# Turning the gate-scaled combine weights by block transposes on VectorE and DMAs

## The chip, the cores and the metric

One core of a Trainium2 chip. The time is device microseconds of one execution, taken as the median of several. The engines are named as the profile names them: PE (TensorE, matmuls), PEld (its weight loads, which run beside the matmuls), DVE (VectorE), ACT (ScalarE), POOL (GpSimd) and SP (SyncE), on whose queue nearly all DMAs are issued.

## What is computed

Three layers, one behind the other: attention with a compressive memory, a soft mixture of experts (32 slots), and a second mixture in which each of 8 experts sees all 2304 tokens, weighted by a balanced gate. The part that matters here, cut from the reference:

```python
# first mixture: combine weights c of 32 slots for each token
x = c @ slot_out                       # 2304 x 512
# second mixture
P = exp(x @ w_gate - max)              # 2304 x 8
for _ in range(8):                     # rows and columns balanced
    P /= P.sum(1); P /= P.sum(0); P *= N / E
for e in range(8):
    out += P[:, e:e+1] * (relu(x @ w1[e]) @ w2[e])
```

## The kernel before

The program runs in stages: attention with the first half of the first mixture (to about 260 us), the slots' experts (to about 320 us), and the second mixture, which takes the rest. Only this last stage is touched.

**What it multiplies.** Since x = c @ slot_out, x @ w1[e] is c @ (slot_out @ w1[e]), a product over 32 slots. prepare_a (L1037) makes slot_out @ w1[e] on TensorE, 32 matmuls per expert. split_a parts it into a rounded high part and the rest, and move_a (L1072) copies these with 16 DMAs of SP's queue into the four bands of 32 partitions of a4s[e]: high, low, high, low. Across it stands c4T (L793), 128 partitions by 2304 tokens: the combine weights c, turned, in the bands high, high, low, low. One matmul over 128 partitions so sums all four partial products.

**The gate.** P is never negative, so P * relu(c @ A) is relu((P c) @ A): the gate is applied by scaling c for each expert. For expert e, scale_c(e, u0, u1) (L1264) multiplies Cw (c with tokens on partitions: tile, slot) by column e of Pr on DVE into cP (L1267), rounds it on ACT to chi (L1272), copies chi twice into c4 (L1276) and writes the remainder cP - chi twice on DVE (L1277). turn_c (L1279) transposes each 128 x 128 tile of c4 on TensorE into a bank of PSUM (L1282), and store_c (L1286) copies the bank on ACT into c4T (L1287). One such step covers four tiles of 128 tokens (two units); the fifth of an expert covers two.

**Units and steps.** A unit is one expert e and 256 tokens u (9 units per expert, 72 in all; g = 9e + u). layer1(g) (L1091) makes the hidden values of a unit with 8 matmuls into the two banks l0 and l1. The second layer of a unit is done with seven products p1 to p7 on quarters of the matrices (the scheme of Strassen and Winograd) in the order p5, p1, p7, p6, p2, p3, p4; each product (L1392) is 12 matmuls at L1402 to L1404, three for each of four strips, high times high, high times low, low times high. hidden(g, k) (L1140) makes the operands: DVE the sums f (L1120) and the low parts a11l, a12l, a22l (L1133), ACT the rounded high parts (L1126), POOL the low parts s1l to s4l (L1137). collect (L1407) adds products from PSUM to accA, accB and accD on DVE (L1418). The products go to banks y0 to y4 in this order, all of one pool with three buffers, so a unit's y0 takes the bank that the unit before used for y2. p7 and p3 share y2, which accB collects. The first five units (RAW) do plain products instead.

**The order** is written out by hand (from L1476 on) for PE, DVE, ACT and POOL: unit by unit, seven steps k each; in a step come product(g, k), at k = 1 also layer1(g + 1), the collecting of the product of the step before, hidden(g + 1, k) for k > 1, and last the functions put `beside` step s = 7g + k (`at(u, k, f, ...)`). SP issues its DMAs in order as their waits allow. With v = 9(e - 1), the first unit of the expert before e, these stand beside the units: load_w1(e) at v, move_a(e) at v + 1, sums and splits of w2 (w_sum, w_hi, w_lo, mostly on POOL) from v + 2 to v + 9, and the steps of c in units v + 6 to v + 10 (L1342), with scale_c at k = 1, turn_c at k = 2, store_c at k = 3. layer1 of the expert's first unit, v + 9, is issued at k = 1 of unit v + 8.

sel (L1014) is a constant selection matrix that only expert 0 uses, in spread_a (L1061).

Of the kernel before, what the change touches and what calls it, by code (L numbers as in the profile page):

```python
# [8 lines left out]
F32 = mybir.dt.float32  # L9
BF16 = mybir.dt.bfloat16  # L10
F32R = mybir.dt.float32r
AF = mybir.ActivationFunctionType
ALU = mybir.AluOpType
# [8 lines left out]
def infini_attention_soft_moe_sinkhorn_moe(  # L22
# [15 lines left out]
    nc = tc.nc  # L38
    B, H, D, S = q.shape
    N, DM = out.shape  # L40
    E = moe2_w1.shape[0]
    FF = moe2_w1.shape[1] * moe2_w1.shape[4]
    NS = moe_phi.shape[2]
    SPE = NS // E
    P = 128
# [3 lines left out]
    KD = DM // P  # L49
# [4 lines left out]
    NTT = N // P  # L54
# [25 lines left out]
    ones = cst.tile([P, P], F32, name="ones")  # L80
# [31 lines left out]
    with ExitStack() as actx:  # L112
        def pool(nm, bufs=1):
# [13 lines left out]
            out=maskw[:, 3 * P :], in_=maskw[:, 3 * P :], compare_op=ALU.is_ge,  # L127
# [6 lines left out]
        for j in range(2):  # L134
            sl = maskt[64 * j : 64 * j + 64]
            nc.gpsimd.affine_select(
                out=sl, in_=sl, compare_op=ALU.is_ge,
# [6 lines left out]
        for i in range(QTB):  # L144
            pr = []
            for nm, w in (("qz", 3 * TAIL), ("qx", 2 * TAIL)):
                t = e2.tile([P, w], F32R, name=f"{nm}{i}")
# [5 lines left out]
        for i in range(2):  # L153
            t = ep[i].tile([P, 2, S], F32R, name=f"klz{i}")
# [77 lines left out]
        for c0, c1 in ((0, 2 * P), (2 * P, S)):  # L232
# [14 lines left out]
            out=gB[:, 1, :], in0=gB[:, 0, :], scalar1=-1.0, scalar2=1.0,  # L247
# [437 lines left out]
        def at(p, n, f, *args):  # L685

            fill.setdefault(3 * NT * p + n, []).append((f, args))
# [84 lines left out]
    with bctx:  # L772
# [20 lines left out]
        c4T = cst.tile([P, 2 * (OB[4] + TAIL)], F32R, tag="pB", name="c4T")  # L793
# [89 lines left out]
        with tc.manual_schedule(engines={mybir.EngineType.PE}):  # L883
            c4 = combine(0)
            first(0)
            for bb in range(1, B):
# [3 lines left out]
                c4 = combine(bb)  # L890
# [18 lines left out]
    mB = ctx.enter_context(tc.tile_pool(name="mB", bufs=1, reuse_waits="tile"))  # L909
# [5 lines left out]
    mD = ctx.enter_context(tc.tile_pool(name="mD", bufs=1, reuse_waits="tile"))  # L915
# [6 lines left out]
    NU = N // UT  # L922
# [80 lines left out]
    def w_lo(e, nm, i, g):  # L1003
# [7 lines left out]
    mD.tile([P, 16], F32, name="gap")  # L1011
    a4s = {0: mD.tile([P, FF], F32R, tag="a4", name="a4", bufs=2)}
    Cw = mD.tile([P, NTT, NS], F32, name="Cw")
    sel = mD.tile([P, 4, 160], F32R, name="sel")  # L1014
    nc.vector.tensor_scalar(
        out=sel.rearrange("p j c -> p (j c)"), in0=ones[:, 0:1].to_broadcast([P, 640]),
        scalar1=0.0, scalar2=None, op0=ALU.mult,
    )

# [8 lines left out]
    a2s, G = {}, {}  # L1028
# [142 lines left out]
    Pr = mB.tile([P, NTT, E], F32, name="Pr")  # L1171
# [2 lines left out]
    m1 = mS.tile([P, 1], F32, name="m1")  # L1174
    m2 = mS.tile([1, 1], F32, name="m2")

    def gate_slots():
        soB = G["soB"] = mB.tile([P, KD, 4, NS], F32, tag="c4", name="soB")
        nc.scalar.activation(out=soB, in_=soR.to_broadcast([P, KD, 4, NS]), func=AF.Copy)

    def gate_weights():
# [80 lines left out]
    cs_ = {}  # L1262

    def scale_c(e, u0, u1):  # L1264
        T0, n = 2 * u0, 2 * (u1 - u0)
        cP = mB.tile([P, 4, NS], F32, tag="cP", name="cP")[:, 0:n]
        nc.vector.tensor_tensor(  # L1267
            out=cP, in0=Cw[:, T0 : T0 + n], in1=Pr[:, T0 : T0 + n, e : e + 1].to_broadcast([P, n, NS]),
            op=ALU.mult,
        )  # L1270
        chi = mB.tile([P, 4, NS], F32R, tag="chi", name="chi")[:, 0:n]
        nc.scalar.activation(out=chi, in_=cP, func=AF.Copy)  # L1272
        c4 = cs_[e, u0] = mB.tile([P, 4, 4, NS], F32, tag="c4", name="c4")
        hb = chi.bitcast(F32).rearrange("p t (o s) -> p t o s", o=1).to_broadcast([P, n, 2, NS])
        cb = cP.rearrange("p t (o s) -> p t o s", o=1).to_broadcast([P, n, 2, NS])
        nc.scalar.activation(out=c4[:, 0:n, 0:2, :], in_=hb, func=AF.Copy)  # L1276
        nc.vector.tensor_tensor(out=c4[:, 0:n, 2:4, :], in0=cb, in1=hb, op=ALU.subtract)  # L1277
# [8 lines left out]
    def store_c(e, u0, u1):  # L1286
        nc.scalar.activation(  # L1287
            out=c4T[:, UT * u0 : UT * u1], in_=G["pc"][:, 0 : UT * (u1 - u0)], func=AF.Copy
        )


    side = {}

    def beside(s, f, *args):
        side.setdefault(s, []).append((f, args))
# [22 lines left out]
    def at(u, k, f, *args):  # L1318
        beside(7 * u + k, f, *args)

    def c_steps(v, e, u0, u1):
        at(v, 1, scale_c, e, u0, u1)
        at(v, 2, turn_c, e, u0, u1)
        at(v, 3, store_c, e, u0, u1)

    for k, u0, u1 in ((-1, 5, 7), (2, 7, 9)):
        for n, f in enumerate((scale_c, turn_c, store_c)):
            at(RAW - 1, k + n, f, 0, u0, u1)
    s = 1
# [9 lines left out]
        at(RAW - 1, 5 + i, w_lo, 0, "T3", i, "P")  # L1339
    for e in range(1, E):  # L1340
        v = NU * (e - 1)
        for i in range(5):  # L1342
            c_steps(v + 6 + i, e, 2 * i, min(2 * i + 2, NU))
        at(v, 0, load_w1, e, e % 2)
        at(v + 3 * (e == 1), 4, load_raw, e)

        at(v + 1, 3 + 2 * (e == 1), prepare_a, e)
        at(v + 1, 4 + (e == 1), split_a, e)
        at(v + 1, 5 + (e == 1), move_a, e)
        for i in range(2):  # L1350
            for n, nm in enumerate(("T1", "T2", "T4")):

                s = 29 + 4 * (3 * i + n) if e == 1 else 7 * (v + 2 + 3 * i + n) + 1
                beside(s, w_sum, e, nm, i, "P")
                beside(s + 2 - (e == 1), w_hi, e, nm, i)
                beside(s + 3 - (e == 1), w_lo, e, nm, i, "P")
            at(v + 6 + i, 2, w_sum, e, "T3", i, "P")
        for nm, k in (("B11", 2), ("T3", 4), ("B21", 6), ("B22", 8)):
            for i in range(2):
                at(v + 8, k + i, w_hi, e, nm, i)  # L1360
                at(v + 8, k + i + (nm[0] == "B" and nm[1] == "2"), w_lo, e, nm, i, "D" if nm == "B22" and i else "P")
# [114 lines left out]
    with tc.manual_schedule(engines={E_.PE, E_.DVE, E_.Activation, E_.Pool}):  # L1476
# [4 lines left out]
        gate_ident()  # L1481
        fill_sel()
        gate_slots()
        prepare_a(0)
        split_a(0)
# [18 lines left out]
        for g in range(len(units)):  # L1504
            nxt = g + 1 < len(units)
            for k in range(7):
                s = 7 * g + k
# [95 lines left out]
```

## Time and profile before

| | us |
|---|---|
| three runs | 1125.75, 1132.69, 1137.99 |
| median | 1132.69 |
| span of the profiled execution | 1137.8 |
| PE busy in it | 1089.2 |
| DVE busy | 858.2 |
| POOL busy | 663.0 |
| ACT busy | 643.7 |

The span runs from the first to the last instruction of the profiled execution. Its own time isn't given beside it; the span lies 0.2 us under the longest of the three runs. Matmuls are pipelined: the profile's duration of one runs from its start to a modelled end and overlaps the next, so what a matmul costs is read from the distance of starts.

### The profile page before, as it was taken

The page shows a single profiled execution, that of the slowest core. Times are in us where ns is not written, and L with a number is a line of the kernel's source. Part 1 is how long each engine was busy: PE and PEld are TensorE (multiplying, and loading weights), DVE is VectorE, ACT ScalarE, POOL GpSimd, SP SyncE. Part 2 cuts the span into 40 slices and gives each one's busy share as a digit, 9 for nine tenths or more (in the row PEclk, how much of TensorE's full clock was granted, in tenths as well). Part 3 has the DMA queues.
Part 4 walks back from the last instruction along what each step waited for, and adds up shares of the span by engine and source line. Part 5 has one row for each costly group of instructions (what it writes and reads, how often), then busy time and mean ns, then how long its engine had stood idle before and what let it go on. Part 6 is the DMA issues. An engine that isn't in the chain of part 4 may idle for free.

```text
span 1137.8 us, 24481 instructions
## 1 busy us (share of the span) xinstructions
PE 1089.2 (96%) x9229; PEld 991.8 (87%) x9229; DVE 858.2 (75%) x1881; ACT 643.7 (57%) x1392; POOL 663.0 (58%) x605
## 2 busy tenths in 40 slices
PE   6979999987999999999999999999999999999998
PEld 4757777774367799999999999999999999999998
DVE  7868898885157467778778877877887787788776
ACT  6868878861153557546555644655564465546442
POOL 4423333300064388587777857776785777678665
PEclk9989999997999999999999999999999999999999
DMA  6567687437932004001300400130040022000111
GB/s 154 162 175 232 198 233 225 116 106 282 419 121 93 1 2 149 20 1 67 95 9 1 149 20 1 56 103 11 1 149 20 1 70 90 10 2 6 52 57 56
DMA packets 42644, 105.70 MB, mean 93 GB/s; under 512 B 8224, under 2 KB 18592, under 8 KB 38432
## 3 DMA queue, kind: packets, MB, share of 16 engines
q1 hardware_dynamic: 42096, 104.07, 28.8%
q8 instruction: 73, 1.20, 0.4%
q14 instruction: 43, 0.35, 0.1%
q10 hardware_dynamic: 432, 0.09, 0.0%
HBM read 95.74 MB, written 4.72 MB: 88 GB/s over the span
## 4 chain that ended last, share of the span: by engine, by line
PE 77%; DVE 7%; DMA 5%; ACT 4%; issue 3%; POOL 2%; SPq 0%; DVEq 0%; ACTq 0%; POOLq 0%
PE y L1402 18%; PE y L1403 18%; PE y L1404 18%; PE l L1096 5%; PE po L447 4%; PE y L1369 2%; PE pt L410 2%; DMA wm<-in_moe_w_dram 2%; PE pa L1043 1%; DMA kd<-in_k_dram 1%; ACT sm L371 1%; DMA w<-in_moe_w_dram 1%; PE pc L1282 1%; DVE sm L367 1%; DMA qp<-in_q_dram 1%
## 5 line engine op out<-in xcount | busy, mean ns | idle before, releaser
L1120 DVE SCALAR_TENSOR_TENSOR f<-l,f 128x512 f32<-128x512 f32 x268 | 184.0, 687 | 61.1 <-ACT a11h L1126 53.1
L1137 POOL TENSOR_TENSOR s1l<-f,s1h 128x512 fp32r<-128x512 f32 x67 | 90.2, 1347 | 157.0 <-ACT s1h L1126 157.0
L1418 DVE TENSOR_TENSOR accA<-accA,y 128x512 f32<-128x512 f32 x125 | 85.4, 683 | 44.3 <-PE y L1404 43.9
L1126 ACT ACTIVATE a12h<-l 128x512 fp32r<-128x512 f32 x72 | 43.2, 600 | 99.2 <-PE y L1404 90.0
L1137 POOL TENSOR_TENSOR s4l<-f,s4h 128x512 fp32r<-128x512 f32 x67 | 87.4, 1305 | 15.8 <-PE y L1403 10.4
L1418 DVE TENSOR_TENSOR accB<-accB,y 128x512 f32<-128x512 f32 x125 | 85.5, 684 | 6.7 <-PE y L1404 0.2
L1137 POOL TENSOR_TENSOR s3l<-f,s3h 128x512 fp32r<-128x512 f32 x67 | 87.1, 1301 | 0.0
L1137 POOL TENSOR_TENSOR s2l<-f,s2h 128x512 fp32r<-128x512 f32 x67 | 86.9, 1297 | 0.0
L1116 ACT ACTIVATE f<-l 128x512 f32<-128x512 f32 x67 | 39.6, 592 | 74.2 <-PE l L1096 73.2
L1096 PE MATMUL l<-c4T,a 128*128 128x256 f32 x576 | 79.1, 280 | 2.1 <-DVE a22l L1133 2.1
L371 ACT ACTIVATE sm<-sm,mn 128x128 f32<-128x128 f32 (+3 forms) x128 | 71.0, 556 | 15.8 <-DVE mn L367 14.5
L1402 PE MATMUL y<-T2h,s2h 128*128 128x256 f32 x268 | 77.6, 290 | 0.0
L1005 POOL TENSOR_TENSOR BB1l<-raw,BB1h 128x512 fp32r<-128x512 f32 x32 | 41.3, 1304 | 61.5 <-ACT BB1h L999 61.5
L1402 PE MATMUL y<-BB2h,s4h 128*128 128x256 f32 x268 | 74.5, 278 | 1.2 <-ACT accD L1416 1.2
L1096 PEld LDWEIGHTS l<-c4T,a 128*128 128x128 f32 x576 | 71.9, 188 | 4.0 <-DVE a22l L1133 3.4
L1402 PE MATMUL y<-BB2h,a12h 128*128 128x256 f32 x268 | 75.0, 280 | 0.0
L1403 PE MATMUL y<-T2l,s2h 128*128 128x256 f32 x268 | 74.6, 278 | 0.0
L1403 PE MATMUL y<-BB2l,s4h 128*128 128x256 f32 x268 | 74.6, 278 | 0.0
L1404 PE MATMUL y<-BB1h,s3l 128*128 128x256 f32 x268 | 74.5, 278 | 0.0
L1404 PE MATMUL y<-T2h,s2l 128*128 128x256 f32 x268 | 74.5, 278 | 0.0
L1402 PE MATMUL y<-BB1h,s3h 128*128 128x256 f32 x268 | 74.4, 278 | 0.0
L1403 PE MATMUL y<-BB1l,s3h 128*128 128x256 f32 x268 | 74.4, 278 | 0.0
(317 smaller groups left out, 4208.6 us busy)
## 6 DMA issues: line engine op xcount, KB each, us to landing
wm<-in_moe_w_dram SPq DMA_DIRECT2D x32, 1024.0 KB, 8.8
raw<-in_moe_w_dram SPq DMA_DIRECT2D x32, 512.0 KB, 4.1
w<-in_moe_w_dram SPq DMA_DIRECT2D x32, 512.0 KB, 4.3
qd<-in_q_dram SPq DMA_DIRECT2D x30, 288.0 KB, 4.4
kd<-in_k_dram SPq DMA_DIRECT2D x30, 288.0 KB, 5.1
qp<-in_q_dram SPq DMA_DIRECT2D x15, 288.0 KB, 3.6
vt<-in_v_dram SPq DMA_DIRECT2D x16, 256.0 KB, 3.1
out_dram<-accB SPq DMA_DIRECT2D x18, 128.0 KB, 1.8
```

The source lines that it names most:

```text
L371: nc.scalar.activation(out=sm[:, 0:n], in_=sm[:, 0:n], func=AF.Exp, scale=-1.0, bias=mnc, accum_out=X.sums[:, i, h : h + 1],)
L447: nc.tensor.matmul(po[64 * h : 64 * h + 64, c0:w], X.vt[:, j, h, :], rhs, start=(j == 0), stop=(j == n - 1),)
L1005: eng(g).tensor_tensor(out=w_tile(e, nm, "l")[:, h], in0=full(e, nm, i), in1=w_tile(e, nm, "h")[:, h].bitcast(F32), op=ALU.subtract,)
L1096: nc.tensor.matmul(ph[:, f, :], a4s[e][:, P * (KH * j + f) : P * (KH * j + f) + P], c4T[:, UT * u : UT * u + UT], start=True, stop=True,)
L1116: nc.scalar.activation(out=f_tile(g, nm), in_=ph(g, nm), func=AF.Relu)
L1120: nc.vector.scalar_tensor_tensor(out=f_tile(g, nm), in0=ph(g, src), scalar=0.0, in1=b, op0=ALU.max, op1=op)
L1126: nc.scalar.activation(out=h_tile(g, nm, "h"), in_=ph(g, nm) if a else FU[g, nm], func=AF.Relu if a else AF.Copy)
L1137: nc.gpsimd.tensor_tensor(out=lo, in0=FU[g, nm], in1=hi, op=ALU.subtract)
L1402: nc.tensor.matmul(o_, hh[:, f, :], wh[:, f, :], start=f == 0, stop=False)
L1403: nc.tensor.matmul(o_, hh[:, f, :], wl[:, f, :], start=False, stop=False)
L1404: nc.tensor.matmul(o_, hl[:, f, :], wh[:, f, :], start=False, stop=f == KH - 1)
L1418: nc.vector.tensor_tensor(out=acc, in0=acc, in1=y, op=ALU.add)
```

## The change

For experts 1 to 7 the five steps of c become two rounds per expert, each of nine tiles of 128 tokens (288 columns). part_c multiplies Cw by the gate on POOL, round_c rounds on ACT, rest_c takes the remainder on POOL, and blocks_c transposes on DVE the 32 x 32 blocks of the rounded part (z = 0) and of the remainder (z = 1) into a tile ct. A block then has its slots on partitions, but the four blocks of a tile of tokens lie in four different bands of partitions. move_c brings them where they belong with 16 DMAs on SP's queue: for each of the four bands z of c4T and each of the four blocks j, 32 partitions with nine pieces of 32 values (128 bytes). Round 0 stands in unit v + 5, at k = 1 to 5, with its moves at k = 6; round 1 in unit v + 6, with its moves at k = 6 of unit v + 7. The tile cw, which holds the operands, is one buffer, and so is ct, which takes the place of sel under the same tag. Expert 0's two steps keep the way of before, in the new tile.

```diff
-    sel = mD.tile([P, 4, 160], F32R, name="sel")
+    sel0 = mD.tile([P, 640], F32, tag="sel", name="sel").bitcast(F32R)
+    sel = sel0.rearrange("p (j c) -> p j c", j=4)
...
+    def cw_tile():
+        return mB.tile([P, 768], F32, tag="cw", name="cw")
...
     def scale_c(e, u0, u1):
         T0, n = 2 * u0, 2 * (u1 - u0)
-        cP = mB.tile([P, 4, NS], F32, tag="cP", name="cP")[:, 0:n]
+        cw = cw_tile()
+        cP = cw[:, 512:640].rearrange("p (t s) -> p t s", s=NS)[:, 0:n]
...
+    NR = NTT // 2
+    WR = NR * NS
+    ct_ = {}
+
+    def part_c(e, r):
+        cw = ct_[e, r] = cw_tile()
+        nc.gpsimd.tensor_tensor(
+            out=cw[:, 0:WR].rearrange("p (t s) -> p t s", s=NS), in0=Cw[:, NR * r : NR * r + NR],
+            in1=Pr[:, NR * r : NR * r + NR, e : e + 1].to_broadcast([P, NR, NS]), op=ALU.mult,
+        )
+
+    def round_c(e, r):
+        cw = ct_[e, r]
+        nc.scalar.activation(
+            out=cw[:, WR : 2 * WR].bitcast(F32R), in_=cw[:, 0:WR], func=AF.Copy
+        )
+
+    def rest_c(e, r):
+        cw = ct_[e, r]
+        nc.gpsimd.tensor_tensor(
+            out=cw[:, 0:WR], in0=cw[:, 0:WR], in1=cw[:, WR : 2 * WR], op=ALU.subtract
+        )
+
+    def blocks_c(e, r, z):
+        if z == 0:
+            ct_[e, r, "t"] = mD.tile([P, 640], F32, tag="sel", name="ct")
+        cw = ct_[e, r]
+        nc.vector.transpose(
+            ct_[e, r, "t"][:, WR * z : WR * z + WR], cw[:, WR * (1 - z) : WR * (2 - z)]
+        )
+
+    def move_c(e, r):
+        ct = ct_[e, r, "t"]
+        to = c4T[:, 0:N].bitcast(F32).rearrange("p (t j n) -> p t j n", j=4, n=32)
+        for z in range(4):
+            for j in range(4):
+                nc.sync.dma_start(
+                    to[32 * z : 32 * z + 32, NR * r : NR * r + NR, j],
+                    ct[32 * j : 32 * j + 32, WR * (z // 2) : WR * (z // 2) + WR].rearrange(
+                        "p (t n) -> p t n", n=32
+                    ),
+                )
...
-    def c_steps(v, e, u0, u1):
-        at(v, 1, scale_c, e, u0, u1)
-        at(v, 2, turn_c, e, u0, u1)
-        at(v, 3, store_c, e, u0, u1)
+    def c_round(v, e, r, w):
+        at(v, 1, part_c, e, r)
+        at(v, 2, round_c, e, r)
+        at(v, 3, rest_c, e, r)
+        at(v, 4, blocks_c, e, r, 0)
+        at(v, 5, blocks_c, e, r, 1)
+        at(w, 6, move_c, e, r)
...
         v = NU * (e - 1)
-        for i in range(5):
-            c_steps(v + 6 + i, e, 2 * i, min(2 * i + 2, NU))
+        c_round(v + 5, e, 0, v + 5)
+        c_round(v + 6, e, 1, v + 7)
         at(v, 0, load_w1, e, e % 2)
```

## Rows read from the trace of the kernel before

**Rows 1.** Page, totals by engine, and shares of the chain that ended last.

```profile
PE 1089.2 (96%) x9229; PEld 991.8 (87%) x9229; DVE 858.2 (75%) x1881; ACT 643.7 (57%) x1392; POOL 663.0 (58%) x605
...
PE 77%; DVE 7%; DMA 5%; ACT 4%; issue 3%; POOL 2%; SPq 0%; DVEq 0%; ACTq 0%; POOLq 0%
```

**Rows 2.** Busy us by stretch: unit 42 (v+6), then expert 5.

```profile
807.08:818.05 10.97, 10.97 (x99) 10.97 (x98) 9.72 (x16) 6.12 (x12) 8.75 (x8) 1.00 0.00 1
...
831.45:930.62 99.17, 99.17 (x881) 97.94 (x879) 79.08 (x129) 54.05 (x102) 72.71 (x57) 1.00 0.15 49
```

**Rows 3.** Waits of DVE, 480 to 1137 us: total, times, longest.

```profile
DVE accA L1418 <- PE y L1404: 41.6, 73, 2.3
```

**Rows 4.** Timeline of weight loads: layer1 (L1096), transposes (L1282). Start, us.

```profile
609.57 0.98 PEld L1096 LDWEIGHTS l<-c4T,a 128*128 128x128 f32 x8
...
611.86 0.45 PEld L1282 LDWEIGHTS pc<-ident,c 128*128 128x128 f32 x4
...
620.46 0.98 PEld L1096 LDWEIGHTS l<-c4T,a 128*128 128x128 f32 x8
...
998.57 1.01 PEld L1096 LDWEIGHTS l<-c4T,a 128*128 128x128 f32 x8
...
1009.41 1.01 PEld L1096 LDWEIGHTS l<-c4T,a 128*128 128x128 f32 x8
...
1096.16 0.98 PEld L1096 LDWEIGHTS l<-c4T,a 128*128 128x128 f32 x8
...
1106.59 0.98 PEld L1096 LDWEIGHTS l<-c4T,a 128*128 128x128 f32 x8
```

**Rows 5.** Groups by shape from 450 us on: busy us, mean ns of one.

```profile
L1267 DVE TENSOR_TENSOR cP<-Cw,Pr 128x128 f32<-128x128 f32 x24 | 16.9, 705 | 0.0
...
L1277 DVE TENSOR_TENSOR c<-cP,chi 128x256 f32<-128x256 f32 x24 | 20.9, 870 | 10.1 <-ACT chi L1272 10.1
...
L1316 POOL TENSOR_TENSOR accD<-accD,accA 128x256 f32<-128x256 f32 x9 | 7.2, 795 | 4.9 <-DVE accA L1418 4.9
```

**Rows 6.** Timeline of DVE: the product cP in two units.

```profile
809.04 1.16 DVE L1267 TENSOR_TENSOR cP<-Cw,Pr 128x128 f32<-128x128 f32 x1
...
831.00 0.28 DVE L1267 TENSOR_TENSOR cP<-Cw,Pr 128x128 f32<-128x128 f32 x1
```

**Rows 7.** Timeline of POOL beside the first of them.

```profile
810.02 1.34 POOL L996 TENSOR_TENSOR raw<-raw,raw 128x512 f32<-128x512 f32 x1
```

**Rows 8.** Timeline of DVE in unit 41 (v+5), from k = 4.

```profile
803.40 0.68 DVE L1133 SCALAR_TENSOR_TENSOR a11l<-l,a11h 128x512 fp32r<-128x512 f32 x1
...
804.36 0.69 DVE L1418 TENSOR_TENSOR accA<-accA,y 128x512 f32<-128x512 f32 x1 [0.28 <-PE y L1404]
...
804.96 0.68 DVE L1120 SCALAR_TENSOR_TENSOR f<-l,f 128x512 f32<-128x512 f32 x1
...
805.72 0.69 DVE L1418 TENSOR_TENSOR accB<-accB,y 128x512 f32<-128x512 f32 x1
```

**Rows 9.** Timeline of TensorE: first product of the next unit.

```profile
806.88 0.28 PE L1402 MATMUL y<-T1h,s1h 128*128 128x256 f32 x1
```

**Rows 10.** move_a's DMAs on SP's queue: issue ns min/median/max, landing.

```profile
L1076 SPq DMA_DIRECT2D a<-ahi x56: 507/588/1484, 351.2 to 967.3; - x56
...
DMA to landing us min/median/max: 1.8/1.9/3.4
```

**Rows 11.** Timeline of SP's queue: move_a twice, load_w1 of expert 6.

```profile
561.59 2.42 SPq L1076 DMA_DIRECT2D a<-ahi  x4
...
569.12 2.49 SPq L1076 DMA_DIRECT2D a<-alo  x4
...
830.28 6.28 SPq L962 DMA_DIRECT2D w<-in_moe_w_dram  x4
```

**Rows 12.** Busy us by stretch, with DMA share (next to last): result stores.

```profile
1060.00:1070.00 10.00, 10.00 (x91) 10.00 (x90) 8.20 (x14) 5.29 (x9) 7.62 (x8) 1.00 0.17 54
```

**Rows 13.** Page, DMA queues: packets, MB, share of 16 engines.

```profile
q10 hardware_dynamic: 432, 0.09, 0.0%
```

More of the change, by code (lines that the diff above doesn't have):

```diff
@@ L1013, in infini_attention_soft_moe_sinkhorn_moe @@
     Cw = mD.tile([P, NTT, NS], F32, name="Cw")
-    sel = mD.tile([P, 4, 160], F32R, name="sel")
+    sel0 = mD.tile([P, 640], F32, tag="sel", name="sel").bitcast(F32R)
+    sel = sel0.rearrange("p (j c) -> p j c", j=4)
     nc.vector.tensor_scalar(
-        out=sel.rearrange("p j c -> p (j c)"), in0=ones[:, 0:1].to_broadcast([P, 640]),
+        out=sel0, in0=ones[:, 0:1].to_broadcast([P, 640]),
         scalar1=0.0, scalar2=None, op0=ALU.mult,
@@ L1175, in infini_attention_soft_moe_sinkhorn_moe @@
     m2 = mS.tile([1, 1], F32, name="m2")
+    def cw_tile():
+        return mB.tile([P, 768], F32, tag="cw", name="cw")
     def gate_slots():
-        soB = G["soB"] = mB.tile([P, KD, 4, NS], F32, tag="c4", name="soB")
+        soB = G["soB"] = cw_tile()[:, 0:512].rearrange("p (c a s) -> p c a s", c=KD, a=4)
         nc.scalar.activation(out=soB, in_=soR.to_broadcast([P, KD, 4, NS]), func=AF.Copy)
@@ L1270, in scale_c @@
         )
[L1271 to L1274, printed above, removed]
+        chi = cw[:, 640:768].rearrange("p (t s) -> p t s", s=NS)[:, 0:n]
+        nc.scalar.activation(out=chi.bitcast(F32R), in_=cP, func=AF.Copy)
+        c4 = cs_[e, u0] = cw[:, 0:512].rearrange("p (t a s) -> p t a s", t=4, a=4)
+        hb = chi.rearrange("p t (o s) -> p t o s", o=1).to_broadcast([P, n, 2, NS])
         cb = cP.rearrange("p t (o s) -> p t o s", o=1).to_broadcast([P, n, 2, NS])
```

## The prediction

> **What bounds the kernel now.** I read the page's totals and its chain first, then the second mixture unit by unit on TensorE, then what DVE, POOL and SP do in the units that the change touches. The page has TensorE busy for 96% of the span and on 77% of the chain [rows 1]. In the second mixture it is fuller still: over expert 5 (831.45 to 930.62 us) it is busy for all 99.17 us, while DVE has 79.08, POOL 72.71 and ACT 54.05 [rows 2]. The waits agree: DVE's largest is for TensorE's results [rows 3], and the view of TensorE's own waits has no row at all from 480 us on. So here a column of TensorE work removed is time removed, as long as the other engines stay ahead.
>
> How long is a unit? Between two starts of layer1 lie 84 products and 8 matmuls of layer1. The stretch 1096.16 to 1106.59 holds nothing else: 10.43 us, or 0.1134 us for each of 92 matmuls. With four turning transposes inside, 609.57 to 620.46, it is 10.89. And 998.57 to 1009.41, again without a transpose, takes 10.84: the same 92 matmuls at 0.118 us each, with no wait shown [rows 4]. So TensorE has two paces here. Slow stretches begin and end at breaks in the stream of products (a group of transposes, the matmuls of prepare_a); I found no rule in the rows for which pace follows a break. Thirty units at the slow pace would be 12.3 us, the whole spread of the runs shown (1125.75 to 1137.99).
>
> **The change part by part.** *Transposes gone.* Experts 1 to 7 have 18 transposes each, 126 in all. Four cost 10.89 - 10.43 = 0.46 us [rows 4], 0.115 each; the mean of 273 ns that a group row would give is a pipelined latency, not a price. Gain: 126 x 0.115 = 14.5 us, all of it on the path. Slow stretches that a transpose set off may go too; other breaks can set them off as well, so I book nothing and leave 4 us either way to the range.
>
> *Work leaving DVE and ACT.* Per full step DVE loses 0.705 + 0.870 us, ACT the copies of L1272 and L1276 and the store of c4T [rows 5]. Neither bounds the units, so nothing is booked, but it leaves DVE idle at step 1, where it was not late before.
>
> *Work added to POOL.* part_c and rest_c work on 288 columns. The nearest row is a 256-column TENSOR_TENSOR, 0.795 us [rows 5]; I take 0.86. Unit v+5 has room: part_c falls into POOL's idle time before s1l. In unit v+6 POOL has 8.75 us today (807.08 to 818.05) [rows 2], and 1.7 more make about 10.5, a full unit. That delays s2l to s4l by at most a microsecond or so, and these are wanted by TensorE several us after they are made: booked at nothing, 1 us per expert (7 in all) if that cover is gone.
>
> *Block transposes on DVE.* Four per expert, each 128 x 288 f32. No such operation is in the trace. From below: 0.28 us, the cP product of 128 columns when POOL leaves it alone. From above: 1.16 us, the same product beside a POOL operation on SBUF [rows 6, 7]. I take 0.4, between the 0.28 for 128 columns and DVE's 0.69 for 512 [rows 8]: it has one input, and the long values of cP are those of a two-input operation. The page "VectorE: DVE Perf Modes" of the Trainium skill, under "The three transpose paths", gives 311 ns for 128x128 in bf16; scaled by columns that would be 0.70 us, an estimate by that page, and would put some 7 us on the sum.
>
> Where do they stand? In unit v+5, blocks_c follows a11l, and accB (the result of p3) must be out of its PSUM bank before TensorE can start the next unit: with three banks, the next y0 takes the bank of y2. In the rows a11l starts at 803.40 and is done near 804.05; accA, f and accB start at 804.36, 804.96 and 805.72 [rows 8]; the next unit's first product starts at 806.88 [rows 9]. With two blocks of 0.4 in between accB ends near 806.75. It just fits: nothing booked for round 0.
>
> *The 16 moves of a round, and who waits for them.* All ct tiles share one buffer, the old one of sel. blocks_c(e, 1, 0) in unit v+6 therefore waits until the 16 DMAs of round 0 have read ct. Its place is one unit after the first block of round 0. The nearest DMAs are move_a's: 0.59 us of issue and 1.9 us from issue to landing [rows 10]; twelve went out between 561.59 and 569.12, 0.627 apart, and SP's queue is empty when round 0 comes [rows 11]. The first can go at 804.5, behind the first block. So the last is issued at 804.5 + 15 x 0.627 = 813.9 and lands at 815.8. On the old timetable DVE would be there at 804.05 + 10.43 = 814.5. DVE stands still for 1.3 us. Queued behind the waiting block on DVE are accA, f(s4), the second block and accB: 0.4 + 0.61 + 0.61 + 0.4 + 0.68 = 2.7 us, so accB ends at 818.5, and TensorE wanted the bank at 806.88 + 10.43 = 817.31. TensorE loses 1.19 us in each expert, 7 x 1.19 = 8.4 us. In general, with c us per move, the loss is 15c - 8.21 us per expert, never under zero.
>
> How sure is c? From below, move_a's shortest issue is 0.507 [rows 10]: no wait at all. From above there is the data: each move is 288 pieces of 128 B, 18 for each of 16 DMA engines, and a completion. The stores of results, 512 packets of 1 KB and 64 completions in 10 us, keep the engines busy for a share of 0.17, or 0.17 x 16 x 10 / 576 = 47 ns a packet [rows 12]; at that price a move takes 19 x 47 = 0.89 us. But the packets of q10, mean size 210 B, show 0.0% of the span, so under 0.05% x 16 x 1137.8 / 432 = 21 ns each [rows 13]: 0.40 us a move, less than its issue. 128 B is nearer to these, so issue decides, and c is 0.627.
> The Trainium skill, page "DMA: Bandwidth & Descriptors", speaks against this under "Specifications": below 512 B the engine reads, modifies and writes. The same page says under "Why small descriptors are slow (HBM only)" that SBUF to SBUF is spared. By the first rule a packet could cost twice; by the second c stays the issue time. The trace has no SBUF-to-SBUF packet under 1 KB; the small loads of q10 show no penalty.
>
> *Round 1* reads nothing that is late: its moves go out at the end of unit v+7 behind the last layer1 of the old expert, and the first reader of tiles 9 to 17 is layer1 of unit v+13. They sit on SP ahead of the next load_w1, which today starts at 830.28 [rows 11], and hold it back some 6 us; prepare_a wants these weights a unit and a half after the load's place, some 15 us, so this is hidden. layer1 of v+13 now waits for DMAs on several semaphores: between 0 and 0.2 us, booked at 0.1, 0.7 in all. If the readers in v+8 waited for round 1 too, each expert would lose over 9 us; the tiles they read are disjoint, and I exclude it.
>
> **Sum.** -14.5 + 8.4 + 0.7 = -5.4 us. The profiled execution spans 1137.8 us; among the runs shown it lies beside the slowest, 1137.99, so about 5 above their median, which fits its long slow-paced stretches. Its sum is 1132.4; taken from the median, 1132.69 - 5.4, rounded: 1127 us.
>
> **The rivals.**
> *One: the moves are done in time.* If c is 0.55 or less, or if the wait is only for the half of ct that is overwritten, DVE does not wait: -14.5 + 0.7 = -13.8, some 1119 us. For it: the first eight moves read the half that the first block overwrites. Against it: a tile is handed on as a whole, and 0.627 was steady over 16 issues of move_a.
> *Two, the slower side: the wait of DVE for round 0 eats the whole gain.* Same place; it decides from the c at which 7 x (15c - 8.21) = 13.8, that is 0.68 us a move, only 8% over what I take. At 0.75 the loss is 21 us and the time 1140; at the 0.89 of 1 KB packets 36 us, so +22 and 1155. For it: pieces of 128 B in such number occur nowhere in the trace. Against it: the 21 ns of q10. By the rule of the Trainium skill's page "DMA: Bandwidth & Descriptors", "Specifications", weighed above, this rival is the one to expect. Blocks of 1.16 us in place of 0.4 would act through the same accB: about 1.3 us in unit v+5 and 1.5 more in v+6, 20 us in all, to 1147.
> *Three: the change does what it says, but pace decides.* Without transposes an expert keeps whichever pace prepare_a leaves it in; two of the five that I looked at stayed slow. If most do, 0.4 us in 20 more units takes 8 us back: 1135.
>
> **How the numbers follow.** Forecast 0.46, rival one 0.20, rival two 0.24, rival three 0.10. One per cent, about what a measurement here can tell from no change, is 11 us: faster means under 1121.4, slower over 1144. Faster: most of rival one (0.17) and the low end of the forecast (0.08), 0.25. Slower: most of rival two, 0.21. The rest, 0.54, lies within. The range reaches down past rival one with 4 us of pace, 1114, and up into rival two, 1150, and leaves out its far end; the forecast's own range is 1119 to 1136.
>
> **What would show it.** In the profile after: no transposes behind pc in experts 1 to 7 and plain units of 10.43 or 10.84; SP rows of 16 moves with their pace (0.63 or more) and landing; on DVE a wait before the second round's first block, named for a DMA, some 1.3 us, seven times or six; right behind it a gap on TensorE at the start of the next unit of 1.2 us. No such gap means rival one; gaps over 2 us mean rival two, and the duration of the blocks tells whether the DMAs or DVE itself is the reason. The forecast is wrong if layer1 shows waits for DMAs of over 1 us, or if POOL becomes the one that TensorE waits for.

## The result, and the profile after

The changed kernel takes 1144.74 us (median of 16 runs, 1134.34 to 1150.51), the kernel before, run in turn with it, 1133.03 (16 runs, 1125.75 to 1140.09). The ratio is 1.0102, 95% interval 1.0074 to 1.0131: slower by 1%, 11.7 us, where 5.4 us less were forecast. In both cases the profiled run is among the longest of its kernel (after: 1150.51, span 1148.4), so the two profiles can be laid side by side.

The page of the changed kernel, totals and the chain's shares, against [rows 1]:

```profile
PE 1091.0 (95%) x9103; PEld 990.2 (86%) x9103; DVE 824.8 (72%) x1839; ACT 614.8 (54%) x1301; POOL 680.7 (59%) x633
...
PE 67%; DVE 10%; POOL 5%; SPq 5%; ACT 5%; issue 4%; DMA 3%; DVEq 0%; ACTq 0%; POOLq 0%
```

The 126 transposes are gone (9229 matmuls became 9103). TensorE's share of the chain fell from 77% to 67%; DVE, POOL, SP's queue and ACT have what it lost. Before, the view had no wait of a matmul from 480 us on, and none of a weight load (PEld) over 0.4 us. Now TensorE has waits of its own. The view of waits of the changed kernel, 450 to 1148 us (who waits and for whom; total, times, longest):

```profile
DVE ct L1324 <- DMA c4T<-ct: 16.8, 6, 3.5
...
PEld y L1454 <- POOL BB2l L1005: 6.0, 11, 0.9
...
PE y L1453 <- DVE accA L1469: 4.7, 5, 1.4
...
PEld l L1097 <- DVE a22l L1134: 3.4, 6, 0.6
...
PEld y L1454 <- DVE BB2l L1005: 2.2, 1, 2.2
```

Two chains stand in these rows. *The first is the one forecast*: DVE waits for the moves of round 0 (2.8 us, six times), and TensorE then for DVE's accA, and once more, in the same unit, for a22l. *The second was not forecast*: at each of the seven changes of expert TensorE waits for BB2l, the low part of a quarter of w2 that POOL (once DVE) makes there.

**The first chain, in the unit of [rows 8] and the next.** The changed kernel on DVE (blocks of both rounds), on SP, and on TensorE:

```profile
807.19 0.47 DVE L1324 STREAM_TRANSPOSE ct<-cw 128x288 f32<-128x288 f32 x1
...
821.53 0.48 DVE L1324 STREAM_TRANSPOSE ct<-cw 128x288 f32<-128x288 f32 x1 [3.42 <-DMA c4T<-ct]
...
821.93 0.65 DVE L1469 TENSOR_TENSOR accA<-accA,y 128x512 f32<-128x512 f32 x1
...
823.49 0.65 DVE L1469 TENSOR_TENSOR accB<-accB,y 128x512 f32<-128x512 f32 x1
```

```profile
807.72 10.85 SPq L1333 DMA_DIRECT2D c4T<-ct  x16
```

```profile
822.70 0.19 PEld L1453 LDWEIGHTS y<-T1h,s1h 128*128 128x128 f32 x1 [1.54 <-issue]
...
826.21 0.88 PEld L1097 LDWEIGHTS l<-c4T,a 128*128 128x128 f32 x7 [0.57 <-DVE a22l L1134]
```

Round 0's first block stands at 807.19, its first move at 807.72, right behind it; the sixteenth is issued 15 distances of 0.683 us later, at 817.96. One unit on, DVE is there at 821.53 - 3.42 = 818.1 and stands until the sixteenth move has landed; accA, queued behind the block, gives TensorE its bank late, and TensorE starts the next unit after an idle 1.54 us. It starts at 822.70, right behind accA (done at 822.58) and before accB has begun. So the bank that a unit's first product takes here is the one that accA empties; that it is the bank of y2, which accB empties, as the kernel's description and the prediction have it, isn't borne out. The view of SP's queue and the groups give the sizes:

```profile
L1333 SPq DMA_DIRECT2D c4T<-ct x192: 585/612/1712, 501.4 to 1039.9; - x192
...
DMA to landing us min/median/max: 2.0/2.0/3.8
```

```profile
L1324 DVE STREAM_TRANSPOSE ct<-cw 128x288 f32<-128x288 f32 x24 | 11.2, 468 | 16.8 <-DMA c4T<-ct 16.8
...
L1316 POOL TENSOR_TENSOR cw<-cw 128x288 f32<-128x288 f32 x12 | 9.8, 816 | 0.0
...
L1303 POOL TENSOR_TENSOR cw<-Cw,Pr 128x288 f32<-128x288 f32 x12 | 8.4, 697 | 0.0
```

A block takes 0.47 us (0.4 was taken), POOL's two products 0.70 and 0.82 (0.86 each), a move 0.61 of issue and 2.0 to its landing (1.9; the last move of two of the six rounds 0 took 3.3 and 3.7). The prediction's c, 0.627, was the distance from one issue to the next. That distance is longer than the issue: 0.689 us in the mean of the six rounds 0 from 450 us on, 0.659 to 0.719 in the single ones. The data isn't what a move costs: over 808 to 812 us this window of the changed kernel has a DMA share (next to last) of 0.32, and 46 GB/s:

```profile
808.00:812.00 4.00, 4.00 (x36) 4.00 (x35) 3.67 (x8) 1.72 (x3) 4.00 (x4) 1.00 0.32 46
```

That is 0.32 x 16 x 4 = 20.5 us of DMA engines for 46 x 4 = 184 KB, or five moves of 304 packets: 13.5 ns for one, under a third of the 47 ns of 1 KB [rows 12], though more than twice as much by the byte. A move's packets so take 0.26 us of the 16 engines, less than its issue. The Trainium skill's page "DMA: Bandwidth & Descriptors" has the engine read, modify and write below 512 B under "Specifications", and spares SBUF to SBUF under "Why small descriptors are slow (HBM only)". The trace doesn't decide between the two, since no run sends the same packets another way. What bounds the moves here is their issue, 0.61 us against 0.26.

**The second chain, at the change from expert 4 to 5.** POOL and the weight loads of TensorE, before (POOL, 829 to 848 us, and weight loads at 848):

```profile
833.95 1.29 POOL L1005 TENSOR_TENSOR BB1l<-raw,BB1h 128x512 fp32r<-128x512 f32 x1 [2.91 <-ACT BB1h L999]
...
844.04 4.00 POOL L1005 TENSOR_TENSOR BB2l<-raw,BB2h 128x512 fp32r<-128x512 f32 x3
848.00 1.75 POOL L1137 TENSOR_TENSOR s1l<-f,s1h 128x512 fp32r<-128x512 f32 x1
```

```profile
848.18 0.19 PEld L1402 LDWEIGHTS y<-BB2h,s4h 128*128 128x128 f32 x1
848.29 0.19 PEld L1403 LDWEIGHTS y<-BB2l,s4h 128*128 128x128 f32 x1
```

and the same of the changed kernel:

```profile
839.15 1.31 POOL L1005 TENSOR_TENSOR BB1l<-raw,BB1h 128x512 fp32r<-128x512 f32 x1 [3.14 <-ACT BB1h L999]
...
849.19 4.25 POOL L1005 TENSOR_TENSOR BB2l<-raw,BB2h 128x512 fp32r<-128x512 f32 x3
853.41 1.28 POOL L1138 TENSOR_TENSOR s1l<-f,s1h 128x512 fp32r<-128x512 f32 x1
```

```profile
851.81 0.19 PEld L1454 LDWEIGHTS y<-BB2l,a12h 128*128 128x128 f32 x1 [0.24 <-POOL BB2l L1005]
...
852.38 0.19 PEld L1453 LDWEIGHTS y<-BB2h,s4h 128*128 128x128 f32 x1
853.49 0.19 PEld L1454 LDWEIGHTS y<-BB2l,s4h 128*128 128x128 f32 x1 [0.92 <-POOL BB2l L1005]
```

Here POOL has eleven operations back to back, from the moment ACT's BB1h comes: 833.95 to 848.04 before, 839.15 to 853.44 after, 14.1 and 14.3 us. BB1h itself hangs on TensorE: on ACT it stands close behind f, and f waits for the results of layer1 (changed kernel):

```profile
837.47 0.60 ACT L1117 ACTIVATE f<-l 128x512 f32<-128x512 f32 x1 [2.55 <-PE l L1097]
...
838.44 0.63 ACT L999 ACTIVATE BB1h<-raw 128x512 fp32r<-128x512 f32 x1
```

In both kernels POOL's row begins 2.5 us after this layer1 does. Before, TensorE wanted the last BB2l at 848.29, 0.25 us behind POOL's end. In the units of that stretch stood two groups of four transposes, 0.92 us, and some 0.4 us of slow pace between them. Without these TensorE is there first, and stands. At four other changes of expert the lead was 0.25 to 0.28 us as well; at the first two from 440 us on it was used up, with breaks of 0.12 and 0.18 us on TensorE. POOL was never idle in this stretch, and the view of waits from 480 us on doesn't name it: cover of 0.25 us looks the same there as cover of 5.

**The pace.** Each product's twelve weight loads give a pitch: near 0.1134 us (10.43 a unit) or near 0.118 (10.84), the two paces of [rows 4]. Counted product by product from 440 us on, those with a break left out: the slow pace has 143 of 420 products before and 263 of 401 after. At 0.41 / 7 us each, the 120 more are 7.0 us. A unit after prepare_a in the changed kernel, weight loads:

```profile
656.16 0.98 PEld L1097 LDWEIGHTS l<-c4T,a 128*128 128x128 f32 x8
...
659.99 1.45 PEld L1044 LDWEIGHTS pa<-w,soT 128*32 128x32 f32 x32
...
668.91 1.01 PEld L1097 LDWEIGHTS l<-c4T,a 128*128 128x128 f32 x8
```

The eight loads of layer1 take 0.98 us at the fast pace and 1.01 at the slow one, so they show it at a glance: fast into prepare_a, slow out of it. Five of the six prepare_a from 450 us on go this way, the first the other way.

**Where 13 us come from.** The second mixture, from its first layer1 to the end of the span, takes 1137.8 - 321.4 = 816.4 us before and 1148.4 - 318.8 = 829.6 after: 13.2 more. By the starts of the weight loads (a break is the distance of two starts, less one pitch), from 440 us on: transposes -14.5 (with the twelve before 440 us; what else differs there cancels to a few tenths); the breaks for accA and a22l behind six rounds 1, 6.3 + 3.9 = +10.2; the breaks for BB2l, +11.9 (1.3 at each of six changes of expert, 4.0 at the one near 546 us, where it is DVE's part that is late and 1.4 of the 4.0 passes at a lower clock); slow pace, some +7.0. That is +14.6. Against it stand 2.0 us of breaks that the kernel before had and the changed one has not: seven of 0.23 to 0.25 us for a22l, and those of 0.12 and 0.18. The sum, 12.6, is within a microsecond of the 13.2.

### The profile page after: what moved, and what is told of

It is laid out like the page before. It is cut to its first block, busy times and chain, and to the rows that moved or that the text cites. A ratio compares the mean times of both kernels' runs of the same rounds, so it can differ in the third digit from the quotient of the medians.

```text
span 1148.4 us, 24415 instructions
## 1 busy us (share of the span) xinstructions
PE 1091.0 (95%) x9103; PEld 990.2 (86%) x9103; DVE 824.8 (72%) x1839; ACT 614.8 (54%) x1301; POOL 680.7 (59%) x633
## 4 chain that ended last, share of the span: by engine, by line
PE 67%; DVE 10%; POOL 5%; SPq 5%; ACT 5%; issue 4%; DMA 3%; DVEq 0%; ACTq 0%; POOLq 0%
PE y L1454 15%; PE y L1453 15%; PE y L1455 15%; PE l L1097 5%; SPq L1333 4%; PE po L447 3%; PE y L1420 3%; POOL BB2l L1005 2%; DMA kd<-in_k_dram 2%; PE pt L410 1%; PE ph L841 1%; DMA c4T<-ct 1%; PE pso L863 1%; ACT sm L371 1%; PE pa L1044 1%
## 5 line engine op out<-in xcount | busy, mean ns | idle before, releaser
L1138 POOL TENSOR_TENSOR s1l<-f,s1h 128x512 fp32r<-128x512 f32 x67 | 87.0, 1299 | 137.2 <-ACT s1h L1127 137.1
L1453 PE MATMUL y<-T1h,s1h 128*128 128x256 f32 x268 | 75.3, 281 | 4.8 <-DVE accA L1469 4.7
L371 ACT ACTIVATE sm<-sm,mn 128x128 f32<-128x128 f32 (+3 forms) x128 | 71.0, 556 | 15.9 <-DVE mn L367 14.6
L1454 PE MATMUL y<-BB2l,a12h 128*128 128x256 f32 x268 | 75.5, 282 | 0.3
L1453 PE MATMUL y<-BB1h,a11h 128*128 128x256 f32 x268 | 75.3, 281 | 0.0
L1454 PE MATMUL y<-T4l,a22h 128*128 128x256 f32 x268 | 75.3, 281 | 0.0
```

Source lines behind the costliest of these rows:

```text
L371: nc.scalar.activation(out=sm[:, 0:n], in_=sm[:, 0:n], func=AF.Exp, scale=-1.0, bias=mnc, accum_out=X.sums[:, i, h : h + 1],)
L1138: nc.gpsimd.tensor_tensor(out=lo, in0=FU[g, nm], in1=hi, op=ALU.subtract)
L1453: nc.tensor.matmul(o_, hh[:, f, :], wh[:, f, :], start=f == 0, stop=False)
L1454: nc.tensor.matmul(o_, hh[:, f, :], wl[:, f, :], start=False, stop=False)
```

## The experiments

The question was which of the two waits and the pace ate the 14.5 us, and whether these were there to be had at all. The theories carry letters in the expectations, which say what each holds.

**Round 1 a unit later, so that its first block comes when the moves of round 0 have long landed:**

```diff
-        c_round(v + 6, e, 1, v + 7)
+        c_round(v + 7, e, 1, v + 7)
```

> Round 1 of each expert stands one unit later (v+7), so that its blocks come two units after those of round 0. Theory A (the lost time is DVE's wait for the 16 moves of round 0, handed on to TensorE through accB): DVE's waits for the moves (16.8 us from 450 us on) fall under 1 us, TensorE's waits for accA (4.7 us) go, and the time falls by 8 to 11 us, to about 1134. Rival B (TensorE's pace is what costs): the waits go just the same, but no break then ends the slow pace before the expert's end, three more units of each expert run at 10.84 in place of 10.43, and the time falls by only 1 to 4 us, to about 1142.

Measured: 1135.35 us (1121.38 to 1143.06, 10 runs), 0.9994 of the kernel before (0.9951 to 1.0038), 9.4 under the changed kernel. In its profile one row of the matmuls' waits is left:

```profile
PE y L1454 <- POOL BB2l L1005: 3.8, 6, 0.7
```

DVE's wait for the moves and TensorE's for accA and a22l are gone with it, so these were the moves' doing. The 9.4 agree with the 10.2 counted in the profile, though the interval of this run leaves some 5 us either way. The other chain stays.

**Both parts of BB22's low half on DVE, not only the second, so that POOL's row at the change of expert is an operation shorter:**

```diff
-                at(v + 8, k + i + (nm[0] == "B" and nm[1] == "2"), w_lo, e, nm, i, "D" if nm == "B22" and i else "P")
+                at(v + 8, k + i + (nm[0] == "B" and nm[1] == "2"), w_lo, e, nm, i, "D" if nm == "B22" else "P")
```

> Both halves of the low part of B22 are made on DVE, one of them on POOL before. Theory C (at the change of expert POOL has eleven operations in one run, 14.3 us, and TensorE, without its transposes, now arrives before the last of them, BB2l): TensorE's waits for BB2l (3.6 us on POOL and 2.0 on DVE from 450 us on) fall under 1 us, and the time falls by 6 to 8 us, to about 1138. If these waits stay or move to DVE's BB2l, C is wrong about POOL; the time then stays at about 1145.

Measured: 1137.5 us (1130.91 to 1144.39), 1.005 (1.0024 to 1.0076), 7.2 under the changed kernel. The 0.92 us before s4 are gone; a shorter wait, for another BB2l, stays, and the first chain is as it was:

```profile
DVE ct L1324 <- DMA c4T<-ct: 16.3, 6, 3.4
...
PE y L1453 <- DVE accA L1469: 4.9, 6, 1.3
...
PE y L1454 <- POOL BB2l L1005: 2.9, 6, 0.5
```

**Both edits:**

> Both edits at once. Theories A and C: no wait of TensorE over 0.5 us per expert is left, and the time is 14 to 18 us under the changed kernel, some 1128, 5 us under the kernel before. Rival B: with no break left between one prepare_a and the next, every unit keeps the pace that prepare_a leaves; if that is the slow one, nine units of 0.41 us are lost in each expert, and the time lies at about 1138.

Measured: 1131.36 us (1125.66 to 1134.84), 1.0000 (0.9977 to 1.0023), 13.4 under the changed kernel. The matmuls' waits are all but gone from the view (1.7 us once, 0.5 once), and still there is no gain over the kernel before; the time lies between the 1128 and the 1138 of the expectation. In its profile 285 of 425 products have the slow pace, 142 more than before: 8.3 us of the 14.5.

**No rounds at all for experts 1 to 7** (their gate scaling is left out; c4T keeps expert 0's):

```diff
-        c_round(v + 5, e, 0, v + 5)
-        c_round(v + 6, e, 1, v + 7)
```

> Experts 1 to 7 are not scaled at all: no round, no move, c4T is left as expert 0 used it, so the output lacks the gate of these experts. Theory C: the wait for BB2l is there all the same, 1.2 us per expert, because it comes from the missing transposes and not from part_c and rest_c on POOL; no wait for accA; time about 1128. Its rival D (part_c and rest_c push POOL back): no wait for BB2l at all; time about 1120. Rival B: most units at 10.84, time about 1135.

Measured: 1131.54 us (1128.8 to 1139.62), 0.9997 (0.9967 to 1.0028). So the transposes removed *at no price* gain nothing that can be measured. This is the run that overturns the sum. TensorE's waits in it:

```profile
PE y L1452 <- POOL BB2l L1005: 3.6, 5, 0.7
...
PE y L1452 <- DVE BB2l L1005: 2.0, 1, 2.0
```

The same, to a tenth, as with the rounds: what exposes POOL is that the transposes are missing, not part_c and rest_c. So the waits are theory C's; the time lies between C's 1128 and B's 1135.

**No rounds, and both halves of B22's low part on DVE** (the gate left out as above):

> The changed kernel without the rounds of c for experts 1 to 7 (so c4T keeps expert 0's scaling and the gate of the later experts is left out), and with both halves of B22's low part on DVE, so that TensorE doesn't wait for POOL at the change of expert. It is the removal of the 126 transposes at no price, with the cover at the change of expert restored. Theory C alone (the lost 14.5 us stand in POOL's row at the change of expert): 7 us under the kernel without rounds, 1124, with plain units at 10.43. Rival H (pace: with the waits gone prepare_a turns the pace over and most experts stay slow until the next one): 1129 to 1132, with three or more of five experts at 10.84 after prepare_a.

Measured: 1128.93 us (1127.46 to 1130.74, 6 runs) beside 1134.3 of the kernel before, 0.9957 (0.9941 to 0.9973). A gain at last, 5.4 us, and rival H's number: 234 of 426 products are slow, 91 more than in the profile of before. The pace is regular here. Between one prepare_a and the next stands a single other break, what is left of the wait for BB2l in the unit ahead of prepare_a: 0.2 us when the pace is slow, 0.75 when it is fast. It turned the pace twice of seven times, from slow to fast (at 544 and 840 us). prepare_a turns it each time: of the six in the profile, four are entered fast and left slow, two entered slow and left fast. One of each, weight loads, from slow to fast and then, one expert later, from fast to slow:

```profile
649.61 1.01 PEld L1097 LDWEIGHTS l<-c4T,a 128*128 128x128 f32 x8
...
653.58 1.45 PEld L1044 LDWEIGHTS pa<-w,soT 128*32 128x32 f32 x32
...
662.26 0.98 PEld L1097 LDWEIGHTS l<-c4T,a 128*128 128x128 f32 x8
```

```profile
746.46 0.98 PEld L1097 LDWEIGHTS l<-c4T,a 128*128 128x128 f32 x8
...
750.29 1.45 PEld L1044 LDWEIGHTS pa<-w,soT 128*32 128x32 f32 x32
...
759.21 1.01 PEld L1097 LDWEIGHTS l<-c4T,a 128*128 128x128 f32 x8
```

**The late round and DVE's half, and prepare_a in two halves of 16 matmuls, a step apart:**

```diff
-    def prepare_a(e):
+    def prepare_a(e, cs=range(4)):
...
-        at(v + 1, 3 + 2 * (e == 1), prepare_a, e)
+        at(v + 1, 2 + 2 * (e == 1), prepare_a, e, (0, 1))
+        at(v + 1, 3 + 2 * (e == 1), prepare_a, e, (2, 3))
```

> As e3_both, and prepare_a of experts 1 to 7 is issued in two halves, a step apart. Theory F: each run of prepare_a's matmuls turns TensorE's pace over, from 0.113 to 0.118 us per matmul or back; two of them leave it as it was, fast after the small wait for BB2l. Then nearly all units take 10.43 us, 5 to 6 experts win 8 x 0.41 us each, 16 to 19 us less 1.5 us for the second break: about 1116. Rival G (the pace that follows a break is chance): some experts slow, some fast, as before, and a time within 3 us of e3_both's 1131. If the halves leave the slow pace every time, 1133.

Measured: 1125.3 us (1113.79 to 1128.22, 8 runs), 0.994 of the kernel before (0.9907 to 0.9974): faster than the kernel before and than the version without the halves, though between F's 1116 and the 1131 of G. Behind both halves the pace is what it was ahead of them (119 of 412 products slow in the profile), but not because a half does nothing: each half turns it, and the second turns it back. Between them stands one product at the other pace. Here the products around it are fast, and this one's eleven distances, from its first weight load to its last, are 0.117 us each:

```profile
451.43 0.19 PEld L1453 LDWEIGHTS y<-T2h,s2h 128*128 128x128 f32 x1 [0.41 <-issue]
...
452.71 0.19 PEld L1455 LDWEIGHTS y<-T2h,s2l 128*128 128x128 f32 x1
```

So it is at all six prepare_a, in whichever pace they are entered. Where the pace stayed slow (two experts), a wait of 2.2 us had turned it.

**The same without the halves, but with four idle transposes of a constant in unit v + 2 (a break as before):**

> As e3_both, and in the unit behind prepare_a stand four transposes of the identity into PSUM that nobody reads, 0.46 us of TensorE in each of 7 experts (3.2 us). If any break turns the pace over or sets it fast, the units behind it are fast: 6 units x 0.41 us in each of 5 to 6 experts, 12 to 15 us won, 1119 to 1122 in all. If a group of transposes leaves the pace as it is, and only prepare_a turns it, 1134.5.

Measured: 1131.56 us (1124.27 to 1138.33), 0.9989 (0.996 to 1.0017). No gain over the version without them (1131.36), and 3 us under the 1134.5 that goes with that. The group of transposes leaves the pace alone here, slow or fast, six times of six; in the kernel before, 15 of the 25 groups of four that have no prepare_a beside them turned it. prepare_a still turns it, from fast to slow four times and back twice.

**No rounds, DVE's half, and the halves of prepare_a** (the gate left out as above):

> As the kernel without rounds and with DVE's half of B22 (gate of experts 1 to 7 left out), and prepare_a in two halves a step apart. Here nothing that was found stands in the way of the 14.5 us. If the transposes cost 0.115 us each and the waits and the pace are all that eats it: 1119, 6 under the version with late rounds, DVE's half and halves, most experts at 10.43. If the price of a removed transpose was too high from the start: no lower than that version, 1125, although no wait of over 0.3 us is left on TensorE and the pace is 10.43 in most experts.

Measured: a median of 1130.31 us, but 12 runs from 1113.44 to 1139.7, a spread of 26.3, eight times that of the version with prepare_a whole (3.3). The view has no wait of a matmul; from start to start 0.2 us for BB2l remain at each change of expert. The profiled run is the longest; its weight loads:

```profile
1051.33 1.01 PEld L1096 LDWEIGHTS l<-c4T,a 128*128 128x128 f32 x8
...
1062.16 1.01 PEld L1096 LDWEIGHTS l<-c4T,a 128*128 128x128 f32 x8
```

All 420 products counted in it are slow (the one between two halves, which is fast, is left out), at 10.84 us a unit, and the granted clock is 1.00 (column before the DMA share):

```profile
900.00:940.00 40.00, 40.00 (x342) 40.00 (x342) 30.22 (x50) 22.30 (x40) 32.08 (x26) 1.00 0.18 67
```

Here the halves cancel each other, and the short waits for BB2l turned nothing, so the run kept the slow pace to its end. 67 units (all but the five plain ones) at 0.41 us are 27.5 us, about the spread. So 1113.44 may be the kernel at the fast pace throughout; that run has no profile, and this isn't shown. Ten of the twelve runs lie between the two, so in most of them the pace must have turned somewhere, if it is what spreads them. The clock doesn't: its mean over the run is 0.986 in the longest and 0.989 in the shortest. Both numbers of the expectation (1119 and 1125) miss: they took the fast pace for granted.

**Do the two cures help elsewhere?** DVE's half in the kernel *before*:

> The kernel before, with both halves of the low part of B22 on DVE. Theory C: with its transposes TensorE came to BB2l just behind POOL, no wait was shown, so nothing is won: within 2 us of the kernel before. If it gains as much as the same edit gained in the changed kernel (7 us), POOL was already the limit there and the transposes have nothing to do with it.

Measured: 1137.62 us (1129.61 to 1144.1), 1.0047 (1.0018 to 1.0077): slower there, where a time within 2 us of the kernel before was expected, and worth 7.2 in the changed kernel. TensorE has waits for DVE's accD in it (1.8 us in five), which explain a part of the loss. So POOL at the change of expert became a limit only by the change. The halves in the *changed* kernel:

> The changed kernel as it is, with prepare_a of experts 1 to 7 in two halves a step apart, nothing else. Theory F: the waits stay (DVE for the moves, TensorE for BB2l), but the units from prepare_a to round 1 keep the fast pace: 6 experts x 5.5 units x 0.41 us, 13 us less, and 1.5 us for the second break: about 1133. Rival G: within 3 us of the changed kernel's 1144.7.

Measured: 1145.13 us (1140.84 to 1146.78, 4 runs), 1.011 (1.0083 to 1.0137), no gain over 1144.74. 97 of 389 products are slow in the profile, against 263 of 401, but the waits have grown:

```profile
PE y L1453 <- DVE accA L1469: 7.0, 6, 1.7
...
PE y L1454 <- DVE BB2l L1005: 4.1, 2, 2.0
```

F's 1133 is missed: a faster TensorE waits longer at the same places. (The profile with 263 is of the longest run of its kernel, so in a median run the pace may have less to give back.) And in the kernel *before*:

> The kernel before, with prepare_a of each expert issued in two halves of 16 matmuls, one step apart, and nothing else changed. Theory F (one prepare_a run turns TensorE's pace over between 10.43 and 10.84 us a unit, two halves leave it as it was; but in this kernel the groups of transposes, the short waits and the full TensorE mix the paces anyway): within 3 us of the kernel before, about 1132. Rival G (the halves by themselves are worth the 6 us that they were worth on top of the late rounds and DVE's half of B22, whatever the rest of the kernel): 1127.

Measured: 1147.38 us (1143.45 to 1153.92), 1.0129 (1.0099 to 1.0158), 13 us slower, against both. Another wait came with it:

```profile
PE pa L1043 <- ACT c4T L1286: 8.5, 6, 1.8
```

The first half, a step earlier, meets the bank that store_c hasn't emptied. This run says nothing on the pace; with the transposes in the kernel the halves aren't the one edit that they were meant to be.

## Why the prediction was wrong

**The step that failed** is the line "Gain: 126 x 0.115 = 14.5 us, all of it on the path", together with its cover, POOL's extra work "booked at nothing, 1 us per expert (7 in all) if that cover is gone". The price of a transpose wasn't the fault. Take 0.0586 us per slow product off each second mixture, so that all are compared at the fast pace (one profile each, so good to some 2 us): before 816.4 - 8.4 = 808.0; without rounds and with DVE's half 805.7 - 13.7 = 792.0. That is 16.0 us, near the 14.5. But this shows only where POOL has been given its lead back. Without DVE's half, no rounds and no transposes, it is 811.1 - 7.8 = 803.3: of 16 us 11 stand in the waits for BB2l and what follows them. The prediction looked for what the change *adds* to POOL, and in units v+5 and v+6. What decided is what it *takes from TensorE* in the units to v+9, where POOL's row begins at a signal that TensorE itself sets off and has a fixed length of 14 us. "A column of TensorE work removed is time removed, as long as the other engines stay ahead" stood in the text; how far they were ahead was not read from the rows, and it was 0.25 us.

**DVE's wait for the moves** was right in its place, but its price came out near the forecast by luck, out of two errors. The term c was too small: the distance of issues was 0.689 us and not 0.627, two rounds landed late, and DVE stood 2.8 us in the mean, not 1.3. And the path from there to TensorE was too long: the bank hung on accA, right behind the block, and not on accB, three operations further, so that in five of six rounds 1.8 us of DVE's wait cost TensorE nothing. Before the unit's first product that leaves 1.05 us in the mean (0.38 to 1.66), where 1.19 was forecast; a22l, which the sum didn't have, takes 0.65 more; and the first expert's round cost nothing. In all 10.2 us, where 8.4 was forecast and the prediction's own formula would give 15 with the true c. Delaying round 1 gave 9.4 back. Rival one fell (the half-buffer isn't told apart). Rival two, the slower side, gave nearly the right time (1140 and more) with half its means: its point of decision, c = 0.68, was passed by a little, but the moves cost 10.2 us, less than the 13.8 or more that it puts there; the rest of the loss is of other causes.

**Pace** was seen and booked at nothing, with rival three at 1135. It came as that rival said ("an expert keeps whichever pace prepare_a leaves it in"), 7.0 us between the profiles, but on top of the waits, not alone. The error was to treat it as noise with a mean that stays: the transposes were among the breaks that mixed it (15 groups of 25 turned it), and what mixed it was removed.

**Right at nothing:** round 1's moves ahead of load_w1 and the blocks in unit v+5 (0.47 each, no wait of TensorE there). Layer1's wait for DMAs, booked at 0.7, has no row. At equal pace the rounds without their two waits (late round and DVE's half, 793.7) stand 1.7 us over no rounds at all (792.0), against the 0.7 booked.

**What stays open** is what the two paces are. Neither the clock nor a wait tells them apart. That prepare_a's matmuls, 32 or 16 in a row, turn one into the other each time, and transposes and short waits only sometimes, was seen but not explained. The medians of runs that had no profile can be put down to pace only by their spread.

## What to carry to other kernels

Before work is taken off the engine that bounds a stage, read for each of its suppliers how long before its use the last piece is ready: a supplier whose row starts at a signal of the bounding engine and has a fixed length gives back only its lead, here 0.28 us of each expert at most. Leave the work out at no price first; if that run isn't faster, moving the work elsewhere won't be either, until what holds that run up is mended too (here with DVE's half, the late round and the halves of prepare_a). And when a kernel's runs spread by 2%, look for a state that persists (here a pitch of 0.1134 or 0.118 us) and for the instruction that turns it, since a change that alters the turning moves the time by more than its own price.

## What the hardware showed that was not expected

- **Two paces at one granted clock.** Matmuls of 256 columns follow each other every 0.1134 or 0.118 us with a granted clock of 1.00 in both. A run of prepare_a's matmuls with 32-column weights turned one into the other each time in the profiles without the transposes of c, 42 of 42 with 32 in a row and 36 of 36 with 16; so 32 as 16 and 16 came out as they went in. Over a whole second mixture it is worth some 27 us, an estimate from 67 units at 0.41.
- **Small packets are cheap from SBUF to SBUF.** 128 B took some 13.5 ns, so the 304 packets of a move cost less on the 16 DMA engines than its 0.61 us of issue.
- **An operation of DVE can take three times its time.** At the change near 546 us in the changed kernel DVE's BB2l took 4.75 us, 1.38 to 1.47 at the other six; POOL worked without a pause from 542.60 to 548.87 beside it. One of over 3 us comes up in five of the ten profiles of the changed kernel and its versions, and in none of the three of the kernel before and its versions. What sets it off is open.

```profile
544.66 4.75 DVE L1005 TENSOR_TENSOR BB2l<-raw,BB2h 128x512 fp32r<-128x512 f32 x1
```

- **A lower clock can come with a wait.** TensorE stood 2.2 us for this BB2l, and then ran some 3 us at a granted clock of 0.50, its lower level, before the clock rose again. That a wait brings this about isn't shown: in the changed kernel with the halves it stood as long, twice, and the clock stayed at 1.00; and at 395.5 us in the changed kernel the clock fell behind a unit of plain products, in which no such wait stands. The two stretches:

```profile
549.60:552.20 2.60, 2.60 (x13) 2.60 (x14) 2.60 (x5) 0.93 (x2) 1.28 (x1) 0.50 0.57 197
...
395.50:398.90 3.40, 3.40 (x18) 3.40 (x17) 1.46 (x3) 2.13 (x4) 3.40 (x4) 0.50 0.00 0
```
